# Long convolution beside a gated matmul: who turns the filter's rows, and over how much work the convolution is spread

## The chip, the cores and the metric

The kernel runs on one core of a Trainium2 chip. The metric is the device time of one execution in microseconds (us), lower is better. The engines named below are PE (matmuls; PEld is its weight load), DVE (element by element), ACT (copies and functions), POOL and SP; POOL, SP and ACT also issue the transfers (DMAs), each from its own in-order queue.

## The reference, cut to what matters

The forward result is `x + s * silu(B)`, with x of 2048 rows by 1024 columns in bf16, `xn` its layer norm, `s` a long convolution and `B` a gated matmul; then all gradients.

```python
xn = _layernorm(x)
# s: shift convolution with 4 taps, product, long causal convolution by FFT, gate
kv = shift(k, shift_k) * v
y  = irfft(rfft(pad(kv)) * rfft(pad(ssm_k)))[:S] + kv * ssm_D     # ssm_k: 1024 x 2048
s  = xn * y
# B: gated matmul, F = 3584
B  = ((xn @ w_gate) * (xn @ w_up)) @ w_down
out = x + s * silu(B)          # and the vector-Jacobian product for ten inputs
```

`ssm_k` is the long filter: one row of 2048 taps for each of the 1024 channels.

## The kernel before, in words

**Layout.** The 2048 rows of the sequence are split by a half c (2), a row u (128) and a residue r (8): row = 1024 c + 8 u + r. A tile with u on the 128 partitions holds sixteen blocks (c, r). The Fourier transform of length 4096 is done as matmuls over u (tables TF, TI) and as sums over r on DVE. The 1024 channels go in eight slices ds of 128.

**The gate/up stage.** `gu_unit` (L629) takes four row blocks at a time of one slab of 256 columns of w_up and w_gate. For each row block PE does eight matmuls of 512 columns into `psg` (L645), of which there are two buffers, ACT copies psg out (L647), and a tick is called. DVE multiplies gate and up into `hN` (L659), PE transposes hN into `tr` (L674, one buffer), ACT copies that to `hT` (L675, two buffers), SP stores it to HTd. Fourteen slabs; the first two partly in a start-up that is not touched.

**The convolution forward** (`conv_forward`, L685) is a generator that emits work slice by slice and yields its estimated DVE cost. For each slice it transforms kv (shifted k times v, from `shift`, once for two slices) and the filter, and multiplies:

- `half` (L764) does the matmuls of a half transform into `psF` (L235, two buffers) and ACT copies them to `SP`.
- `transform` (L771) does the sums on DVE; kind 0 is kv for ds > 0, kind 1 the filter. The list EIGHT picks the eight-residue form for slices 0 and 7.
- `h_rows(ds, c)` (L722) makes the filter's rows ready: `load_h` has brought the slice's 128 channels by 2048 taps into the lower half of U[5] (`hrow`, channels on partitions, tap order c, u, r). For each r PE transposes every eighth tap (L731, L733), eight transposes into `tr`, and ACT copies the eight blocks to `hx` with a scale (L734). It is called for slice ds + 1 in the middle of slice ds's kind 1 transform, once for each c. The next slice's transform reads hx.
- `product` (L333) multiplies the spectra, `inv_dft` or `inv8` brings the product back into HX on DVE, and `tail` (L743) does the last matmuls into `psY` (L438 or L449), from where ACT copies to `yf` and POOL stores to YFd.

`shift` uses U[7] for its products.

**The pace.** `make_pump` runs the generator up to a given share of F_TOTAL. `tick` (L916) is called after each row block and pumps to a share that grows in proportion to (count + 6.5) / (NT + 3.5), with NT = 24 * 8 + 14 = 206. The count starts at -5 and there are 200 row blocks, so it is 195 at the stage's end. DVE's instructions of the convolution keep their emitted order (`pinned`, L207); otherwise a scheduler places the instructions on each engine.

**The first pair.** With the gate/up stage done, the assertion at L981 demands that all forward transforms have been emitted, and psF's space is given to `psbm`. `bm_first` (L973) does 28 chunks fc for the first two row blocks of `h @ w_down` (L969): 112 matmuls of 512 columns. After fc = 5, 7, ... 27 it calls `tick(0.74)`. Between the first four chunks and the rest, pools are released and opened: `ub` holds U[8] to U[11], `bw` and `mh` hold later tiles. Then the loads of the last three down weights (`load_wd(4..6)`, L1252) and of the next pair's operand (`load_ht(1)`) are issued, and `drain` empties the generator. `gate` (L1187) does the elementwise work of each row block on ACT and DVE; it reads YFd. Row block accumulators use three PSUM tiles in turn.

The rest of the kernel (seven more pairs, then all gradients) is bound to the same engines in other ways and isn't edited.

Of the kernel before, what the change touches and what calls it, by code (L numbers as in the profile page):

```python
# [10 lines left out]
ACT = mybir.ActivationFunctionType  # L11
ALU = mybir.AluOpType
AX = mybir.AxisListType
BF16 = mybir.dt.bfloat16
# [5 lines left out]
def build_kernel(  # L20
# [11 lines left out]
    nc = tc.nc  # L32
    P = 128
# [3 lines left out]
    NB = S // P  # L37
    DC = D // P
    NF = F // P
# [3 lines left out]
    WSC = 2.0 / 2048.0  # L43
# [16 lines left out]
    def ld(out, in_):  # L60
        return nc.sync.dma_start(out=out, in_=in_)
# [182 lines left out]
    def net(w):  # L244
        w -= 0.95 * pe_us[0]
        pe_us[0] = 0.0
        return w
# [12 lines left out]
    def fwd4_buf(wp):  # L260
        return wp.tile([P, 2, 2, 4, 256], F32, name="W", tag="W")
# [242 lines left out]
    U = [ua.tile([P, 4096], BF16, name=f"U{i}") for i in range(8)]  # L504

    def u8(i, pat="p (a x) -> p a x", **kw):
        return U[i][:].rearrange(pat, **kw)
# [170 lines left out]
    h_out = []  # L678
# [1 line left out]
    INV8 = (2, 4, 6)  # L680
    SHIFT_W = 8 * 2.3

    conv_state = {"forward": True}

    def conv_forward():  # L685
        S_ = conv_state
# [11 lines left out]
        def load_h(ds):  # L698
            hrow = U[5][:, 0:2048].rearrange("p (c u r) -> p c u r", c=2, r=8)
            cld(U[5][:, 0:2048], A_ssm_k[ds * P:(ds + 1) * P, :])  # L700
            S_["h", ds] = hrow
# [20 lines left out]
        def h_rows(ds, c):  # L722
            if ds == 8:
                return
            hrow = S_["h", ds]
            if c == 0:
                S_["hx"] = cf.tile([P, NB, P], BF16, name="hx")
            pe_us[0] += 0.47
            ps = ps_tr.tile([P, 8, P], BF16, name="tr")
            with tc.issue_after(tr_ln[0].ins):  # L730
                nc.tensor.transpose(ps[:, 0, :], hrow[:, c, :, 0], ident[:])  # L731
            for r in range(1, 8):
                nc.tensor.transpose(ps[:, r, :], hrow[:, c, :, r], ident[:])  # L733
            nc.scalar.activation(S_["hx"][:, 8 * c:8 * c + 8, :], ps[:], ACT.Copy, scale=WSC)  # L734
            if c == 1:
                h_out.append(ds)
                if ds + 1 < 8:
                    load_h(ds + 1)

        def kvs(ds):  # L740
            return S_["kvt", ds // 2][:, :, ds % 2 * P:(ds % 2 + 1) * P]
# [18 lines left out]
        cf = pool("cf", 1)  # L760
# [9 lines left out]

        def transform(ds, kind, sp, X, C, ahead, step):  # L771

            if (ds, kind) in EIGHT:
                W = fwd4_buf(cs)[:].rearrange("p a b c x -> p (a b c) x")
                for n, w in enumerate(fwd8(sp, X, W, C, ahead)):
                    if n in (0, 2, 4, 6):
                        step()
                    yield net(w)
                return
            W = fwd4_buf(cs)  # L780
            fwd4_sums(W, sp[0], 0)
# [12 lines left out]
            yield net(2.4)  # L794
# [9 lines left out]
        for ds in range(8):  # L804
            yield 0.5
            if ds % 2 == 1 and ds < 7:
                with tc.issue_after(S_["kst"].ins):
                    for c in range(2):
                        load_kv(ds // 2 + 1, c)
            D0 = Dz[:, ds * P:(ds + 1) * P]  # L810
            sph = []
            KX = cx.tile([P, 16, 256], BF16, name="KX")
            HX = cs.tile([P, 16, 256], BF16, name="HX", bufs=2)
            own_room = lambda X: X[:].rearrange("p a x -> p (a x)").bitcast(F32).rearrange("p (a x) -> p a x", a=8)[:, 0:4]
            eight = (ds, 1) in EIGHT
            if ds == 0:
                yield from transform(0, 1, sp, HX, own_room(KX), lambda i: sph.append(half(0, kvs(0), i)), nop)
            else:
                yield from transform(ds, 0, sp, KX, own_room(HX), lambda i: sph.append(half(ds, S_["hx"], i, D0)), nop)
                S_["kst"] = st(KFd[ds], KX[:])  # L820
            next(tl, None)
            room = cf.tile([P, 4, 256], F32, name="room", tag="hx")[:] if eight else None
            yield from transform(ds, int(ds > 0), sph, HX if ds else KX, room, nop1 if eight else lambda c: h_rows(ds + 1, c),
                                 lambda: next(tl, None))
            if ds == 0:
                S_["kst"] = st(KFd[0], KX[:])
            if eight:
                h_rows(ds + 1, 0)
            turned(HX, 1, 0, 1)
            yield 1.3  # L830
            if eight:
                h_rows(ds + 1, 1)
            if ds == 7:
                cf.release()
                S_["forward"] = False
            st(HFd[ds], HX[:])
            yield from product(KX, HX, KX, cs, False, 0)
            if ds % 2 == 1 and ds < 7:
                yield from shift(ds // 2 + 1)
            sp = []  # L840

            def ahead():
                if ds < 7:
                    sp.append(half(ds + 1, kvs(ds + 1), len(sp)))
            yield from (inv8 if ds in INV8 else inv_dft)(KX, HX, cs, ahead if ds % 2 == 0 else None, ahead)
            if ds % 2 == 1:
                ahead()
            S_["G", ds] = HX
            tl = tail(ds)
# [27 lines left out]
    last, root, xst = layer_norm(*xs[0])  # L877
    xsts = [xst]
    for i, (b0, n, x4) in enumerate(xs):
        chunk[0] = i  # L880
        if i + 1 < len(xs):
            with tc.issue_after(last.ins):
                last, root, xst = layer_norm(*xs[i + 1])
# [27 lines left out]
    ps_cv = pool("ps_cv", 2, space=PSUM)  # L911
    pump, drain = make_pump(conv, F_TOTAL)
    cnt = [-5]
    NT = 24 * 8.0 + 14

    def tick(by=1):  # L916
        cnt[0] += by
        if cnt[0] == -4:
            pump((SHIFT_W + 4.05) / F_TOTAL)
        if cnt[0] >= -2:  # L920
            pump((SHIFT_W + (F_TOTAL - SHIFT_W) * (cnt[0] + 6.5) / (NT + 3.5)) / F_TOTAL)

# [26 lines left out]
    for hf in range(2):  # L949
# [5 lines left out]
        for sl in range(NSL - 2, NSL):  # L955
            for b0 in (8 * hf, 8 * hf + 4):
                gu_unit(sl, b0, 4, slabs[sl - NSL + 2], tick)
            if (hf, sl) == (1, NSL - 2):
                wd_ld = load_wd(3)
# [13 lines left out]
    def bm_first(fcs):  # L973
        for fc in fcs:
            for i in range(2):
                mm = bm_mm(pss[i], lambda fc: HT0[fc // 16][:, fc % 16], i, fc)
            if fc % 2 == 1 and fc > 4:
                tick(0.74)
        return mm

    assert not conv_state["forward"]  # L981
# [4 lines left out]
        flush()  # L986
    for p_ in (ps_gu, fg, fw):
        p_.release()

    ub = pool("ub", 1, side="right")
    U += [ub.tile([P, 4096], BF16, name=f"U{i}") for i in range(8, 12)]
    bw = pool("bw", 2, side="right")
    mh = [pool("mh0", 1, side="right")]
    ps_bx = pool("ps_bx", 1, space=PSUM)
# [181 lines left out]
    bpump, bdrain = make_pump(conv_backward(), C_TOTAL)  # L1179

    ddo = const.tile([P, 8], BF16, name="ddo")
    WD += [u8(j, a=4) for j in (2, 3, 9)]
    DBMT = [u8(q, a=DC) for q in (10, 8, 4, 5)]

    tr_name = ["tr"]
# [44 lines left out]
        return wdt  # L1230

    def load_ht(bp):
        if bp == 1:
            two_ = [u8(10, a=16), u8(8, a=16)]
            for f0, f1 in ((0, 16), (16, 24), (24, 28)):
                last = ld(two_[f0 // 16][:, f0 % 16:f0 % 16 + f1 - f0], ht_rows(bp, f0, f1))
            return (lambda fc: two_[fc // 16][:, fc % 16]), last
        ht = mh[bp % 2].tile([P, NF, 256], BF16, name="ht")
        for f0, f1 in ((0, 24), (24, 28)):
            last = ld(ht[:, f0:f1], ht_rows(bp, f0, f1))  # L1240
        return (lambda fc: ht[:, fc]), last
# [7 lines left out]
            ld(t, GUd[k // 2, k % 2])  # L1249
            DGU[k] = t  # L1250

    for j in range(4, 7):  # L1252
        wd_ld = load_wd(j)
    with tc.issue_after(wd_ld.ins):
        ht1 = load_ht(1)
    with tc.issue_after(ht1[1].ins):
        ht2 = load_ht(2)
    bm_first(range(4, NF))
    drain()
    PIN[0] = False  # L1260
    mh.append(pool("mh1", 1, side="right"))
# [93 lines left out]
    def load_h(sl):  # L1355
        h = u8(HSL[sl % 3], "p (a b f) -> p a b f", a=2, b=NB)
        ld(h, Hd[sl])
        hs[sl] = h
# [64 lines left out]
    for k in range(NSL - 1):  # L1423
# [19 lines left out]
        for f in range(2):  # L1443
# [7 lines left out]
            f0 = k * SLW + f * P  # L1451
# [180 lines left out]
```

## Time and profile before

| what | value |
|---|---|
| median of 3 runs | 1929.33 us (1928.45 to 1930.34) |
| profiled execution, its own time | 1929.26 us |
| its span, first to last instruction | 1927.5 us |
| granted TensorE clock, mean | 1.000 |
| PE idle in the span | 15.6 us (1927.5 - 1911.9) |
| gate/up stage, paced part | some 70 to 518 us |
| first pair of row blocks | 518 to 545 us |

How to read it: the page gives busy time by engine, then the span in 40 slices (48 us each) with a digit for the busy tenths. Answers of the trace give waits (who waited for whom, total us, times, longest), busy time in chosen stretches, and timelines (start, duration, engine, line, what). A line such as `psF<-kv,TF` names the tile written and the tiles read. PE's matmuls are pipelined: their durations overlap, and work is better counted by the distance between their starts.

### The profile page before, as it was taken

Reading aid. Unit: us, or ns where it says so; the run is one execution under the profiler, and the core shown is the slowest. Engines: PE = TensorE matmul, PEld = TensorE weight load, DVE = VectorE, ACT = ScalarE, POOL = GpSimd, SP = SyncE. Lnnn points to the kernel's source line nnn. Section 1 sums busy time; section 2 is a strip of 40 time slices with the busy share of each in tenths; the row PEclk is TensorE's granted clock in tenths of the full one; section 3 lists DMA queues with packets and bytes.
Section 4 is the critical chain, followed back from the end, with each engine's and each line's share of the span. In section 5 each row is a group of like instructions: output and inputs, shape, how many; then the busy total and the mean of one; then the engine's idle time right before and its main releaser. Section 6 shows DMA issues by size and latency. Waiting matters only on the chain.

```text
span 1927.5 us, 27456 instructions
## 1 busy us (share of the span) xinstructions
PE 1911.9 (99%) x10978; PEld 1030.1 (53%) x10978; DVE 1542.5 (80%) x1695; ACT 638.7 (33%) x943; POOL 331.0 (17%) x461
## 2 busy tenths in 40 slices
PE   8999999999999999999999999999999999999999
PEld 5555555555444456665666666664444444444444
DVE  8999999999937555888899999999996404287884
ACT  5854555555432233343222322222222102011113
POOL 5121212111112210000122131021211101011111
PEclk9999999999999999999999999999999999999999
DMA  9776866758899987666788698575786999889975
GB/s 297 264 259 221 257 211 229 234 197 266 270 278 312 298 291 257 209 201 218 264 243 264 234 247 263 201 262 186 224 253 174 143 205 217 168 178 188 189 180 171
DMA packets 451360, 444.43 MB, mean 231 GB/s; under 512 B 268800, under 2 KB 371612, under 8 KB 436768
## 3 DMA queue, kind: packets, MB, share of 16 engines
q1 hardware_dynamic: 394848, 243.36, 47.9%
q0 software_dynamic: 40064, 169.95, 27.6%
q10 hardware_dynamic: 16320, 29.36, 4.2%
q8 instruction: 86, 1.41, 0.3%
q14 instruction: 42, 0.34, 0.1%
HBM read 194.00 MB, written 185.64 MB: 197 GB/s over the span
## 4 chain that ended last, share of the span: by engine, by line
PE 80%; DVE 15%; issue 3%; DMA 1%; ACT 1%; SPq 0%; POOL 0%; DVEq 0%; ACTq 0%; POOLq 0%
PE psb L1340 20%; PE psx L1470 20%; PE psb L1323 10%; PE psbm L969 10%; PE psb L1418 9%; PE psg L645 6%; DVE W L213 4%; DVE KX L213 3%; DVE HX L213 2%; DVE m L213 2%; PE psF L235 1%; DVE U L213 1%; DVE hN L213 1%; PE psY L438 1%; PE psY L1116 1%
## 5 line engine op out<-in xcount | busy, mean ns | idle before, releaser
L645 PE MATMUL psg<-wslab,U 128*128 128x512 bf16 x1792 | 407.2, 379 | 2.5 <-DMA wslab<-in_B_w_gate_dram 1.6
L1340 PE MATMUL psb<-U,U 128*128 128x512 bf16 x1792 | 397.1, 379 | 0.0
L1470 PE MATMUL psx<-U,dgut 128*128 128x512 bf16 x1536 | 332.8, 379 | 0.0
L1470 PEld LDWEIGHTS <-dgut 128*128 128x128 bf16 x1792 | 175.3, 98 | 211.4
L1340 PEld LDWEIGHTS <-U 128*128 128x128 bf16 x1792 | 175.2, 98 | 198.0
L645 PEld LDWEIGHTS <-U 128*128 128x128 bf16 x1792 | 172.5, 98 | 187.7 <-issue 2.3
L1323 PE MATMUL psb<-wdt,U 128*128 128x256 bf16 x1792 | 205.6, 273 | 0.0
L1323 PEld LDWEIGHTS <-U 128*128 128x128 bf16 x1792 | 175.3, 98 | 29.2
L1418 PE MATMUL psb<-U,U 128*128 128x512 bf16 x816 | 177.1, 379 | 0.0
L213 DVE TENSOR_TENSOR W<-W 128x1024 f32<-128x1024 f32 (+1 forms) x174 | 171.6, 1003 | 3.7
L1345 ACT CAST wb<-psb 128x512 bf16<-128x512 f32 x112 | 65.6, 586 | 315.1 <-PE psb L1340 313.4
L969 PE MATMUL psbm<-U,ht 128*128 128x512 bf16 x672 | 145.7, 379 | 0.0
L1418 PEld LDWEIGHTS <-U 128*128 128x128 bf16 x896 | 87.5, 98 | 104.5
L647 ACT CAST gut<-psg 128x512 bf16<-128x512 f32 x156 | 91.6, 588 | 119.4 <-PE psg L645 118.9
L1502 ACT ACTIVATE dx_t<-dxn 128x1024 bf16<-128x1024 f32 x15 | 15.9, 1057 | 324.6 <-DVE dxn L213 324.6
L1168 DVE SCALAR_TENSOR_TENSOR dkp<-dkT,kT 128x1024 bf16<-128x1024 bf16 (+2 forms) x64 | 78.4, 1224 | 38.9 <-DMA dkT<-DKSHd 36.9
L969 PEld LDWEIGHTS <-ht 128*128 128x128 bf16 x672 | 65.6, 98 | 78.6
L213 DVE TENSOR_TENSOR U<-U,dht 128x2048 bf16<-128x2048 bf16 x56 | 68.3, 1221 | 46.8 <-ACT dht L1325 46.7
L1325 ACT CAST dht<-psb 128x512 bf16<-128x512 f32 x112 | 65.7, 587 | 116.3 <-PE psb L1323 116.3
L66 POOL DMA_DIRECT2D Hd<-hN x54 | 37.3, 691 | 297.5 <-DVE hN L213 295.0
L213 DVE TENSOR_TENSOR dxn<-psx,dxna_t 128x1024 f32<-128x1024 f32 x15 | 18.3, 1222 | 78.2 <-PE psx L1470 73.3
L1449 ACT CAST wbs<-psb 128x512 bf16<-128x512 f32 x51 | 29.9, 586 | 145.7 <-PE psb L1418 134.2
(237 smaller groups left out, 2452.0 us busy)
## 6 DMA issues: line engine op xcount, KB each, us to landing
U<-GUd SPq DMA_DIRECT2D x28, 1024.0 KB, 8.2
DGd<-U SPq DMA_DIRECT2D x28, 1024.0 KB, 5.8
GUd<-gut ACTq DMA_DIRECT2D x39, 512.0 KB, 5.7
out_dram<-wb SPq DMA_DIRECT2D x112, 128.0 KB, 4.0
U<-Hd SPq DMA_DIRECT2D x14, 1024.0 KB, 6.0
Hd<-hN POOLq DMA_DIRECT2D x54, 256.0 KB, 4.2
HTd<-hT SPq DMA_DIRECT2D x52, 256.0 KB, 4.1
ht<-HTd SPq DMA_DIRECT2D x6, 1536.0 KB, 10.1
```

The lines of the kernel that those rows point to most:

```text
L66: ins = nc.gpsimd.dma_start(out=out, in_=in_)
L213: pinned(V.tensor_tensor(o, a, b, op))
L645: gu_mm[0] = nc.tensor.matmul(ps[:], XNT[q][:, dc, qi * P:(qi + 1) * P], w[:, dc].rearrange("p a f -> p (a f)"), start=(dc == 0), stop=(dc ...
L647: nc.scalar.copy(out=gut[:, :, i], in_=ps[:].rearrange("p (a f) -> p a f", a=2))
L969: mm = nc.tensor.matmul(ps[:, dh * 512:(dh + 1) * 512], ht(fc)[:, i * P:(i + 1) * P], WD[fc // 4][:, fc % 4, dh * 512:(dh + 1) * 512], sta ...
L1168: ins = V.scalar_tensor_tensor(prod[:].rearrange("p r d -> p (r d)")[:, lo:H], dkT[:, 0, lo:H], 1.0, kT[:, 0, 13 + m + lo:13 + m + H], op0 ...
L1323: nc.tensor.matmul(ps[:, x * SLW:(x + 1) * SLW], DBMT[2 * hf + g][:, dc, (b % 4) * P:(b % 4 + 1) * P], wdt[:, dc, :], start=(dc == 0), sto ...
L1325: nc.scalar.copy(out=dht[:, 2 * e:2 * e + 2].rearrange("p b f -> p (b f)"), in_=ps[:])
L1340: nc.tensor.matmul(ps[:], XN[b // 4][:, b % 4, dc * P:(dc + 1) * P], dgus[b // 8][:, :, b % 8], start=(b == 0), stop=(b == NB - 1))
L1345: nc.scalar.copy(out=wb[:, dc % 2].rearrange("p a f -> p (a f)"), in_=ps[:])
L1418: nc.tensor.matmul(ps, h[:, f, b, :], DBM[b // 4][:, b % 4, dh * 512:(dh + 1) * 512], start=(b == 0), stop=(b == NB - 1))
L1470: nc.tensor.matmul(ps[:, dh * 512:(dh + 1) * 512], t[n][:, f, i * P:(i + 1) * P], WGU[n][:, f, dh * 512:(dh + 1) * 512], start=(n == 0 and ...
```

## The change

Three parts go together. From the second slice on, `h_rows` does not use PE: ACT reads the filter's rows from U[5] with a step of eight taps and writes them, scaled and in the order c, r, u, into the lower half of U[7]; after the second half SP issues one transposing DMA of that 128 x 2048 tile into hx. Slice 0 keeps the transposes. The convolution is paced over NT = 24 * 8 + 20 ticks; all fourteen odd chunks of the first pair tick by a whole 1. And the flag that allows psF's space to be reused is set when slice 7's last transform begins, not when it ends; a second flag, `filters`, still marks its end, and the code does chunks of the first pair until it is reached before the pools that need the convolution's space are opened. The loads of the last down weights and of the second pair's operand are issued ahead of that loop.

```diff
-    conv_state = {"forward": True}
+    conv_state = {"forward": True, "filters": True}
...
             hrow = S_["h", ds]
+            if ds > 0:
+                by_r = U[7][:, 0:2048].rearrange("p (c r u) -> p c r u", c=2, r=8)
+                nc.scalar.activation(by_r[:, c], hrow[:, c].rearrange("p u r -> p r u"), ACT.Copy, scale=WSC)
+                if c == 1:
+                    S_["hx"] = cf.tile([P, NB, P], BF16, name="hx")
+                    nc.sync.dma_start_transpose(out=S_["hx"][:], in_=U[7][:, 0:2048])
+                    h_out.append(ds)
+                    if ds + 1 < 8:
+                        load_h(ds + 1)
+                return
...
         def transform(ds, kind, sp, X, C, ahead, step):
+            if ds == 7 and kind == 1:
+                S_["forward"] = False
...
                 cf.release()
-                S_["forward"] = False
+                S_["filters"] = False
...
-    NT = 24 * 8.0 + 14
+    NT = 24 * 8.0 + 20
...
-            if fc % 2 == 1 and fc > 4:
-                tick(0.74)
+            if fc % 2 == 1:
+                tick()
...
     U += [ub.tile([P, 4096], BF16, name=f"U{i}") for i in range(8, 12)]
+    WD += [u8(j, a=4) for j in (2, 3, 9)]
+    for j in range(4, 7):
+        wd_ld = load_wd(j)
+
+    def load_ht1():
...
+    with tc.issue_after(wd_ld.ins):
+        ht1 = load_ht1()
+    fc_ = 4
+    while conv_state["filters"]:
+        bm_first([fc_])
+        fc_ += 1
     bw = pool("bw", 2, side="right")
...
-    for j in range(4, 7):
-        wd_ld = load_wd(j)
-    with tc.issue_after(wd_ld.ins):
-        ht1 = load_ht(1)
...
-    bm_first(range(4, NF))
+    bm_first(range(fc_, NF))
```

`load_ht1` has the body that `load_ht` had for its second pair.

More of the change, by code (lines that the diff above doesn't have):

```diff
@@ L994, in build_kernel @@
     U += [ub.tile([P, 4096], BF16, name=f"U{i}") for i in range(8, 12)]
+    WD += [u8(j, a=4) for j in (2, 3, 9)]
+    for j in range(4, 7):
+        wd_ld = load_wd(j)
+    def load_ht1():
+        two_ = [u8(10, a=16), u8(8, a=16)]
+        for f0, f1 in ((0, 16), (16, 24), (24, 28)):
+            last = ld(two_[f0 // 16][:, f0 % 16:f0 % 16 + f1 - f0], ht_rows(1, f0, f1))
+        return (lambda fc: two_[fc // 16][:, fc % 16]), last
+    with tc.issue_after(wd_ld.ins):
[4 more added lines that the diff above has]
+        fc_ += 1
     bw = pool("bw", 2, side="right")
@@ L1181, in build_kernel @@
     ddo = const.tile([P, 8], BF16, name="ddo")
-    WD += [u8(j, a=4) for j in (2, 3, 9)]
     DBMT = [u8(q, a=DC) for q in (10, 8, 4, 5)]
@@ L1232, in load_ht @@
     def load_ht(bp):
[L1233 to L1237, printed above, removed]
         ht = mh[bp % 2].tile([P, NF, 256], BF16, name="ht")
```

## The prediction

> **What bounds the kernel now.** I read the span in slices first, then the waits of TensorE, then busy time by stretch, then single stretches of the timeline. The page says that PE never rests and that DVE is as full as PE in the first quarter of the span only:
>
> ```profile
> PE 1911.9 (99%) x10978; PEld 1030.1 (53%) x10978; DVE 1542.5 (80%) x1695; ACT 638.7 (33%) x943; POOL 331.0 (17%) x461
> ...
> PE   8999999999999999999999999999999999999999
> ...
> DVE  8999999999937555888899999999996404287884
> ```
>
> A busy PE is modelled, so I also took the distance from one matmul's start to the next: 0.216 us for 512 columns, 0.109 us for 256, 0.056 us for a 128-column transpose. From 60 to 560 us nothing else shows except three gaps. They are the whole list of waits of PE in that stretch:
>
> ```profile
> PE psF L235 <- DVE kv L213: 3.1, 2, 1.9
> PE tr L674 <- DVE hN L213: 1.7, 1, 1.7
> ```
>
> So in this stage two engines run neck and neck, and PE is stopped where it catches up with DVE. By stretch (columns: PE, PEld, DVE, ACT, POOL, clock, DMA share, GB/s):
>
> ```profile
> 300.00:400.00 100.00, 99.82 (x632) 56.76 (x631) 99.07 (x89) 56.37 (x81) 18.86 (x26) 1.00 0.71 231
> 400.00:425.00 25.00, 23.12 (x145) 13.31 (x144) 24.76 (x18) 13.32 (x18) 2.61 (x4) 1.00 0.64 208
> 475.00:500.00 25.00, 23.25 (x137) 12.20 (x136) 24.79 (x33) 13.60 (x21) 2.98 (x6) 1.00 0.82 269
> 525.00:550.00 25.00, 25.00 (x134) 12.83 (x133) 4.39 (x3) 2.91 (x6) 0.02 (x1) 1.00 0.83 225
> ```
>
> DVE is 99% busy up to 525 us, then rests for over 20 us while PE does the first pair of row blocks (L969): that is the room the change wants to use. The clock is 1.00 throughout. After 550 us PE has no wait worth naming, so what is won before 550 us should reach the end.
>
> **Removed: fourteen halves of eight transposes.** In the timeline of PE around slice 7 (start, duration, what):
>
> ```profile
> 433.25 0.22 PE L731 MATMUL tr<-ident,U 128*128 128x128 bf16 x1
> 433.30 0.60 PE L733 MATMUL tr<-ident,U 128*128 128x128 bf16 x7
> 433.74 1.67 PE L645 MATMUL psg<-wslab,U 128*128 128x512 bf16 x7
> 435.25 0.22 PE L731 MATMUL tr<-ident,U 128*128 128x128 bf16 x1
> 435.31 0.61 PE L733 MATMUL tr<-ident,U 128*128 128x128 bf16 x7
> 435.75 2.54 PE L645 MATMUL psg<-wslab,U 128*128 128x512 bf16 x11
> ```
>
> From the group's first start to the next L645 matmul is 0.49 and 0.50 us. Seven slices times two halves times 0.50 is 7.0 us. The matmul ahead of a group is also followed later than usual (0.22 to 0.50 us where 0.216 is normal); over the fourteen halves that adds 0.8 us. **7.8 us** of PE's queue goes, all of it in the stage where PE is full.
>
> **Moved: the pace of the convolution.** The pump releases convolution work in proportion to (ticks + 6.5) / (NT + 3.5). At the last matmul group of the gate/up stage the count is 195, so the share released falls from 201.5/209.5 = 0.962 to 201.5/215.5 = 0.935. F_TOTAL works out to some 408, so about 10 us of DVE work moves out of the stage into the first pair, and all along the stage DVE owes less at each PE position. Is that enough? I summed, along the order in which the instructions stand in each program, PE's start distances up to a matmul that reads DVE's result, and DVE's start distances (medians by shape from this trace) up to the instruction that makes it. PE's sum minus DVE's, before and after, in us:
>
> - kv of slice 2: 173.8 - 177.0 = -3.2; after 177.0 - 177.6 = -0.6
> - kv of slice 4: 285.2 - 289.9 = -4.7; after 290.4 - 291.1 = -0.7
> - kv of slice 6: 396.6 - 403.3 = -6.7; after 405.4 - 403.9 = +1.5
> - worst hN transpose: 474.5 - 482.8 = -8.3; after 463.4 - 465.0 = -1.6
> - last slice's inverse, read by L449: after 519.9 - 520.9 = -1.0
>
> The first, -3.2, passed without a wait in the trace (PE had lost that much more in its start-up). Each further step down, 1.5, 2.0 and 1.6, is a stall, against 1.2, 1.9 and 1.7 us of idle time in the trace: the bookkeeping gives the three waits, so I trust it for the changed order. There nothing lies below -3.2. **4.8 us** of stalls (3.1 + 1.7) goes.
>
> **What is late next.** DVE's last inverse step ends at 529.4 us now (its timeline: start 527.06, two instructions, 2.36). The four tails that read it (L449) start at 541.96 us now, at 525.1 in PE's sum. In the changed order they stand behind all 112 matmuls of the pair instead of 104, at 519.9. That is 541.96 - 5.2 - 4.8 - 0.8 = 531.2 us, 1.8 us behind DVE. DVE will no longer be always late, so it will itself wait for some SP copies: the tightest, kv of slice 6, has 1.8 us of room today and its sum falls from 9.6 to 2.1 while PE's lag shrinks by 6, which is a wait of 1 to 1.5 us. I leave **0.6 us** of PE waiting at the tails. Behind them the gates wait for YFd's round trip as now; pair 2's accumulators are needed only some 14 us later, and ht1's loads and the last down weights (issued at 530 us now, the second read at 540) keep their place relative to PE.
>
> **Added on ACT.** The fourteen copies of L734 (1.02 us, from PSUM, contiguous) become fourteen from SBUF that pick every eighth element. No ACT row reads with such a step. Nearest in engine and size is L734 itself, 1.02 us; the same rows read with that step slowed PE's weight load from 98 to 148 ns, a factor of 1.5, giving 1.53; POOL's reordering at L1120, 4.15 us for 2048 elements, gives 2.07 for 1024.
>
> ```profile
> L733 PEld LDWEIGHTS <-U x112: 142/148/155, 63.5 to 435.6; 128*128 128x128 bf16 x112
> ...
> L734 ACT ACTIVATE hx<-tr x16: 1016/1024/1042, 65.2 to 436.0; 128x1024 bf16<-128x1024 bf16 x16
> ...
> L1120 POOL COPY ho<-yl x8: 3731/4147/4683, 1252.5 to 1489.6; 128x2048 bf16<-128x2048 bf16 x8
> ```
>
> In the built order both copies stand side by side for slices 1, 3, 4 and 7. With two psg buffers ACT may hold the queue for 2 x 1.73 - 2 x 0.59 = 2.3 us before PE stops (a group of eight is 1.73 us, its copy 0.59). Two at 1.02 fit and cost nothing; two at 1.53 cost 0.8 us, at 2.07 1.8 us, so 3.1 or 7.4 us over four slices. I take 1.02, the row of the same engine and size, and keep 7.4 for the range. A gain is excluded, since ACT is 56% busy here and bounds nothing. The copies' wait for U[7] is behind the shift's last product, which ACT has already passed when it copied the same slice's kv spectrum.
>
> The Trainium skill speaks against this part: SBUF — State Buffer, Door 1: The DMA port swizzle, says that an access which crosses to a new 16-byte line pays a penalty, and eight bf16 is just such a line. The weight load's 148 against 98 ns agrees with it; it names no size for ACT, so by it the sum would lie somewhere in my upper half.
>
> **Added on SP and the DMA engines.** Seven transposes of 512 KB. The row of the same size is wdt, from DRAM:
>
> ```profile
> L1229 SPq DMA_TRANSPOSE wdt<-in_B_w_down_dram x14: 1307/4266/7498, 652.4 to 1203.1; - x14
> ...
> DMA to landing us min/median/max: 4.2/7.9/16.0
> ```
>
> None reads SBUF, so I keep 1.3 to 10.0 us on SP (the longest transpose row, at L1404) and 4 to 16 us to land. hx is read 26 to 49 us after today's PE transposes, so the landing is hidden; the shortest distance, 26 us, is slice 1's, and only 10 + 16 us together would reach it. The queue they are put into carries the hT stores and the slabs. hT has two buffers and a copy every 7.4 us, so a store may end 14.7 us after its copy; behind a 4.3 us transpose and with 4.1 us of its own it ends after 8.4, behind 10.0 after 14.1. Both fit. Seven times 512 KB is 3.7 MB in a stretch that moves some 105 MB at a DMA share of 0.7: nothing.
>
> **Sum.** The profiled execution took 1929.3 us (span 1927.5 and 1.8 around it), as the median of the runs shown, 1929.3. 7.8 + 4.8 - 0.6 = 12.0, so **1917.3 us**, 0.6% faster.
>
> **Rivals.** (1) *DVE comes late at the tails.* It has 1.8 us of room. If each of seven slices loses one copy's 1.0 us because SP's spectrum copy stands behind a reordering copy, DVE ends 7 us later, PE waits 5.2 us, and the time is 1922. For it: DVE is 99% busy and has no reserve. Against: the tight SP copies are those of kv, and the reordering stands behind them. (2) *The gain is eaten.* Copies at 2.07 us (7.4 us) together with the late DVE (5.2 us) give 1930: no change. POOL's row speaks for it; against it, the two prices have to come together. (3) *SP is held, slower.* If a transpose out of SBUF holds SP longer than any row shows, the hT store behind it is late, ACT stops at the next hT copy, and with it the psg copies. ACT stops from 14.7 - 4.1 = 10.6 us of issue, PE from 12.9, and the gain is gone at 12.9 + 12/7 = 14.6 us. At twice the longest row, 19.9 us, PE loses 7.0 us seven times: 1966. Against: SP spends 367 us of waiting for hT, so it is mostly free; for: no row has this source.
>
> **Chances.** Forecast 0.57, rival 1 0.19, rival 2 0.10, rival 3 0.14. The forecast itself spans 1914 (8.2 + 5.3 + 1 for the runs' spread, no new wait) to 1920 (copies at 1.53). To leave out no more than 2 in 10 the range takes in rival 1 and the dear copies alone (1924.7), with the runs' spread: 1913.5 to 1926.5. Faster by over 0.2%, about what a measurement of this kernel can tell from no change (below 1925.5): 0.76; within it 0.10; slower 0.14.
>
> **What would show it.** L733 falls from 112 to 14 matmuls; PE waits for kv and hN vanish and PE's busy time drops by 7 to 8 us; the first psbm matmul, at 518.4 us now, starts near 506; the 525 to 550 stretch has DVE no longer resting from its start relative to the pair; the reordering copies take 1.0 us; the transposes take 4 us on SP. Wrong would be: a copy of 2 us or more, psF waiting for hx, L645 waiting for ACT, hT copies waiting for a store, or L449 waiting for HX by more than 2 us.

## The result, and the profile after

The changed kernel takes 1956.47 us (median of 4 runs, 1955.83 to 1962.85), the kernel before 1928.93 on the same chip: 1.0151 times, interval 1.0138 to 1.0163. Where 12 us less were forecast it is 27.5 us more. The profiled execution has a span of 1954.1 us, 26.6 more than before.

The page of the changed kernel, the lines that answer to those of before. PE has lost 112 transposes and yet is busy longer, and ACT does not show what it did: 33% before and after.

```profile
PE 1917.2 (98%) x10866; PEld 1026.5 (53%) x10866; DVE 1542.9 (79%) x1695; ACT 652.9 (33%) x943; POOL 329.2 (17%) x461
...
PE   8999999999999999999999999999999999999999
...
DVE  8989899898968554888799899999997303488873
```

PE's waits from 60 to 600 us (who waits for whom, total us, times, longest). The waits for DVE (two lines before, for kv and for hN) are gone, as forecast. In their place PE waits eight times for ACT, to take over an accumulator (`psg`, `psY`):

```profile
PE psg L645 <- ACT gut L647: 9.6, 3, 4.7
PE psg L645 <- ACT U L647: 8.2, 3, 4.6
PE psY L449 <- ACT yf L759: 8.0, 2, 4.9
```

By stretch (PE, PEld, DVE, ACT, POOL, clock, DMA share, GB/s), the same four as before:

```profile
300.00:400.00 100.00, 92.89 (x552) 51.76 (x551) 87.89 (x77) 57.16 (x74) 16.94 (x24) 0.95 0.66 207
400.00:425.00 25.00, 25.00 (x143) 12.53 (x142) 24.83 (x22) 11.48 (x19) 3.76 (x5) 1.00 0.82 278
475.00:500.00 25.00, 25.00 (x143) 12.77 (x141) 24.73 (x25) 10.33 (x16) 2.74 (x5) 1.00 1.02 338
525.00:550.00 25.00, 25.00 (x143) 12.80 (x141) 24.33 (x34) 11.26 (x18) 4.27 (x6) 1.00 0.69 216
```

Between 300 and 400 us PE does 552 instructions where it did 632, DVE is 88% busy where it was 99%, and the clock is 0.95 on average. So both engines that ran neck and neck now stand still for something else.

**Where the 26.6 us lie.** The first `psbm` matmul starts at 518.4 us before and at 545.0 after: all of the difference, since from there to the end both take 1409.1 us. Up to there, by the distance of matmul starts: stops of over 0.3 us grow from 5.3 us (three) to 27.1 us (eight), +21.8. After most of them the granted clock is 0.5 for 3.4 or 6.8 us, 30.7 us in six stretches, in which the starts of 512-column matmuls lie 0.43 us apart and not 0.216; I sum the excess to 12.7 us. The transposes' 7.8 us are gone. 21.8 + 12.7 - 7.8 = 26.7, which is 0.2 more than the start of `psbm` moved.

Seven of the eight stops stand where the seven pairs of copies stand in ACT's queue. The eighth, 3.0 us at 500 us, does not: the last copy started at 439.54, and here ACT had waited for the store of an hT buffer:

```profile
501.39 1.01 ACT L675 COPY hT<-tr 128x1024 bf16<-128x1024 bf16 x1 [5.42 <-DMA HTd<-hT]
```

One stop, read in two timelines (start, duration, engine, what, in brackets the idle time before it and what ended it). ACT first, then PE:

```profile
105.28 0.59 ACT L647 CAST U<-psg 128x512 bf16<-128x512 f32 x1 [1.14 <-PE psg L645]
105.76 1.02 ACT L675 COPY hT<-tr 128x1024 bf16<-128x1024 bf16 x1
111.23 2.02 ACT L728 ACTIVATE U<-U 128x1024 bf16<-128x1024 bf16 x1 [4.46 <-DMA hx<-U]
113.15 0.57 ACT L647 CAST U<-psg 128x512 bf16<-128x512 f32 x1
113.62 2.03 ACT L728 ACTIVATE U<-U 128x1024 bf16<-128x1024 bf16 x1
```

```profile
105.52 3.62 PE L645 MATMUL psg<-wslab,U 128*128 128x512 bf16 x16
113.78 4.48 PE L645 MATMUL psg<-wslab,U 128*128 128x512 bf16 x13 [4.64 <-ACT U L647]
```

A reordering copy for slice 2 stands in ACT's queue at 107 us, though its rows go on only at 146.37, when the next transposing DMA is issued. It may not write U[7] yet: the transposing DMA of slice 1's rows, issued at 104.65, still reads it. That one had itself waited on SP for the space of hx: in slice 0 DVE works there (a tile `room` has the same place), and its last instruction on it ended at 104.62. The six later ones go out when the last matmul that reads hx has ended (0.03 us after it). ACT waits 4.46 us and works 2.02; both psg buffers fill in the meantime, and PE stands. The clock of the stretch behind it, and of the one behind the stop at 342 us:

```profile
105.00:109.00 4.00, 4.00 (x26) 2.02 (x24) 4.00 (x6) 1.50 (x2) 1.78 (x3) 1.00 0.94 165
109.00:114.00 5.00, 0.36 (x2) 0.10 (x1) 3.10 (x3) 2.77 (x3) 0.00 (x0) 0.95 1.04 420
114.00:117.00 3.00, 3.00 (x8) 1.06 (x7) 0.85 (x2) 2.12 (x2) 0.00 (x0) 0.52 0.33 135
...
347.00:352.00 5.00, 4.61 (x15) 2.16 (x15) 0.21 (x1) 3.43 (x4) 1.15 (x1) 0.50 0.18 57
```

The fourteen copies together, what ended ACT's idle time before them, and SP's transposing DMAs:

```profile
L728 ACT ACTIVATE U<-U x14: 1997/2060/2140, 83.1 to 439.5; 128x1024 bf16<-128x1024 bf16 x14
...
  DMA hx<-U: 9.2, 3
  DVE U L213: 6.8, 3
```

```profile
L731 SPq DMA_TRANSPOSE hx<-U x7: 1417/2037/3033, 104.7 to 466.5; - x7
...
DMA to landing us min/median/max: 4.3/5.3/6.9
```

A copy takes 2.06 us, twice what I took, and its queue place costs ACT another 16.0 us of waits. The transposing DMAs, 1.4 to 3.0 us on SP, lie near the cheap end of my bounds.

### The profile page after: what moved, and what is told of

Same layout as the page of the kernel before. It is cut to its first block, busy times and chain, and to the rows that moved or that the text cites. A ratio compares the mean times of both kernels' runs of the same rounds, so it can differ in the third digit from the quotient of the medians.

```text
span 1954.1 us, 27246 instructions
## 1 busy us (share of the span) xinstructions
PE 1917.2 (98%) x10866; PEld 1026.5 (53%) x10866; DVE 1542.9 (79%) x1695; ACT 652.9 (33%) x943; POOL 329.2 (17%) x461
## 4 chain that ended last, share of the span: by engine, by line
PE 85%; DVE 7%; DMA 3%; issue 2%; ACT 2%; POOL 0%; SPq 0%; ACTq 0%; DVEq 0%; POOLq 0%
PE psb L1354 20%; PE psx L1484 20%; PE psg L645 10%; PE psb L1337 10%; PE psbm L981 10%; PE psb L1432 9%; PE psF L235 2%; DVE U L213 2%; DVE KX L213 1%; DVE W L213 1%; DMA HTd<-hT 1%; DMA hx<-U 1%; DVE m L213 1%; ACT U L728 1%; PE psY L438 1%
## 5 line engine op out<-in xcount | busy, mean ns | idle before, releaser
L645 PE MATMUL psg<-wslab,U 128*128 128x512 bf16 x1792 | 417.0, 386 | 20.8 <-ACT gut L647 10.2
L213 DVE TENSOR_TENSOR W<-SP 128x1024 f32<-128x1024 f32 x64 | 74.4, 1219 | 14.0 <-ACT SP L257 10.9
```

The source lines that it names most:

```text
L213: pinned(V.tensor_tensor(o, a, b, op))
L645: gu_mm[0] = nc.tensor.matmul(ps[:], XNT[q][:, dc, qi * P:(qi + 1) * P], w[:, dc].rearrange("p a f -> p (a f)"), start=(dc == 0), stop=(dc ...
```

## The experiments

Two theories. **A**: ACT is the cause: the copies' length and their waits hold its queue, and the stops halve the clock. **S** (the prediction's third rival): SP and the transfers are the cause, through hT's stores. The first two expectations also name **B**, the later pace is the cause, and C, which is S under an earlier name. Edits are against the changed kernel, ratios against the kernel before with their intervals.

**1. The parts alone.** First the pace with PE's transposes kept for every slice:

```diff
-            if ds > 0:
+            if ds > 8:
```

> All filter rows are again transposed by PE, the pace over 212 ticks, the early release of psF's space and the loop of the first pair stay. Theory A (the loss is ACT's: reordering copies of 2.06 us that also stand in its queue waiting for U[7], PE stops, and its clock falls to half after the long stops): no reordering, so no loss; the wait list of PE shows no psg waits on ACT, the clock stays 1.000, the waits for kv and hN (4.8 us) shrink, and the time is 1922 to 1927 us. Theory B (the loss is the later pace: tails, gates or the pair come late): the loss stays, 1945 us or more. Theory C (the transposing DMAs hold SP's queue or load the DMA engines): as A.

Measured 1924.28 us, 0.9971 (0.9959 to 0.9982). Of PE's waits from 60 to 580 us one line is left; before it was 3.1 + 1.7:

```profile
PE psY L438 <- ACT yf L759: 0.4, 1, 0.4
```

`psbm` starts at 512.9, 5.5 us earlier, against 4.8 forecast for this part. Then the turning alone:

```diff
-    NT = 24 * 8.0 + 20
+    NT = 24 * 8.0 + 14
...
-            if fc % 2 == 1:
-                tick()
+            if fc % 2 == 1 and fc > 4:
+                tick(0.74)
```

> ACT and the DMA turn the rows as in the changed kernel, but the pace is that of before (206 ticks, twelve ticks of 0.74 in the first pair). Theory A: the stops by ACT stay (22 us of idle, some 12 us of half clock), 7.8 us of transposes stay away, so 1948 to 1960 us. Theory B: back near 1922 us, for the pace was the fault. Theory C: as A.

Measured 1948.18 us, 1.0093 (1.0076 to 1.0110). So the turning does the harm. The parts do not add up: with it the new pace makes things 8.3 us worse (1956.5 against 1948.2), without it 5.1 us better. PE's wait for hN is still there (2.8 us), the two for kv are not: a stop by ACT gives DVE time, so that there is little left for the pace to win. In the two profiled runs `psbm` starts 7.0 us apart; 1.8 us of that are stops (27.1 against 25.3) and 4.9 half clock (30.7 us of it against 20.5). Why the later pace meets more half clock was not tested; three stops of the earlier pace, of 2.4 to 3.2 us from start to start, passed at full clock (the last section has to do with this).

**2. ACT or SP.** Without the copies; the DMA turns U[5] as it lies:

```diff
-                nc.scalar.activation(by_r[:, c], hrow[:, c].rearrange("p u r -> p r u"), ACT.Copy, scale=WSC)
...
-                    nc.sync.dma_start_transpose(out=S_["hx"][:], in_=U[7][:, 0:2048])
+                    nc.sync.dma_start_transpose(out=S_["hx"][:], in_=U[5][:, 0:2048])
```

> The changed kernel without ACT's fourteen copies: the transposing DMA reads the rows as they lie in U[5], so order and scale of the filter are left out and the run is for its time alone. ACT is then free of the new work, and SP and the DMA engines carry all of theirs. Theory A (ACT is held by the copies, their 2.06 us and their 16 us of waits for U[7], and the stops cost half clock on top) expects 1917 to 1923 us: the run with the pace alone, 1924.3, less the 7.8 us of transposes, plus up to 6 us for the tails. Theory S (the seven transposing DMAs are slow among the other transfers and hold SP, so that an hT copy on ACT waits for its store) expects 1928 to 1945 us, with ACT hT waiting for HTd in stops of 5 us and more.

And the copies without a use, PE transposing as before (`return` and the DMA are taken out of the branch, so that it falls through to the transposes):

```diff
-                if c == 1:
-                    S_["hx"] = cf.tile([P, NB, P], BF16, name="hx")
-                    nc.sync.dma_start_transpose(out=S_["hx"][:], in_=U[7][:, 0:2048])
-                    h_out.append(ds)
-                    if ds + 1 < 8:
-                        load_h(ds + 1)
-                return
```

> PE transposes all slices as in the kernel before, with the changed pace (1924.3 us), and ACT does the fourteen stepped copies into U[7] besides, which nothing reads; no transposing DMA. Theory A expects 1935 to 1950 us: fourteen times 2.06 us in ACT's queue, pairs of them at 4.1 us against the 2.3 us that ACT may hold PE's two psg buffers, and a wait for the shift's products of some 7 us; stops over 2.3 us draw half clock. Theory S expects no more than 1930 us, since no transfer is added.

Measured 1921.13 us, 0.9949 (0.9930 to 0.9969), and 1949.66 us, 1.0094 (1.0070 to 1.0118). For the changed kernel this decides for A: seven transposing DMAs on SP and no copies, 3.2 us less than the pace alone; fourteen dead copies and no transposing DMA, 25.4 us more. PE's waits without the copies, then with the dead copies:

```profile
PE psg L645 <- ACT gut L647: 3.6, 1, 3.6
PE psF L235 <- ACT SP L295: 0.2, 1, 0.2
PE psF L235 <- ACT SP L257: 0.2, 1, 0.2
```

```profile
PE psg L645 <- ACT gut L647: 13.4, 6, 4.7
PE psg L645 <- ACT U L647: 5.8, 5, 3.2
```

The dead copies wait as well, 6.3 us for the shift's products and 3.9 for the load of the rows, so the 25.4 us are not length alone.

**3. Why the copies are dear: length.** Contiguous copies at the same place (order left out):

```diff
-                nc.scalar.activation(by_r[:, c], hrow[:, c].rearrange("p u r -> p r u"), ACT.Copy, scale=WSC)
+                nc.scalar.activation(U[7][:, 1024 * c:1024 * c + 1024], U[5][:, 1024 * c:1024 * c + 1024], ACT.Copy, scale=WSC)
```

> The changed kernel, but ACT copies the rows in the order they lie (contiguous read and write, the reordering is left out, so the filter's values are wrong); place, waits and transposing DMAs are as in the changed kernel. If the length of the stepped copy is the main fault: copies of 1.0 us, two of them fit the 2.3 us that are free, and the time falls to 1918 to 1930 us. If the wait for U[7] (16 us in ACT) is the main fault: ACT still stops for it, and the time stays at 1938 us or more, with the clock still falling to half after three to five stops.

And a contiguous read with a stepped write (128 elements):

```diff
-                nc.scalar.activation(by_r[:, c], hrow[:, c].rearrange("p u r -> p r u"), ACT.Copy, scale=WSC)
+                nc.scalar.activation(by_r[:, c].rearrange("p r u -> p u r"), hrow[:, c], ACT.Copy, scale=WSC)
```

> The changed kernel, but ACT reads the rows in order and writes with a step of 128 elements, so the same reordering is done on the writing side. Theory A with a dear read: the copies take 1.0 us, ACT is held for 2 us less per slice, the waits for U[7] stay (16 us), and the time lies between 1935 and 1950 us. If a stepped write costs as much as a stepped read, the copies take 2 us and the time stays near 1956 us.

Measured 1939.78 us, 1.0048 (1.0035 to 1.0062), and 1991.44 us in a single run, above both values expected for it. The copies' group in the one and in the other:

```profile
L728 ACT ACTIVATE U<-U x14: 1039/1057/1090, 85.4 to 427.5; 128x1024 bf16<-128x1024 bf16 x14
...
  DMA hx<-U: 9.5, 3
  DVE U L213: 6.8, 3
```

```profile
L728 ACT ACTIVATE U<-U x14: 4745/4766/5088, 83.2 to 474.6; 128x1024 bf16<-128x1024 bf16 x14
```

A contiguous copy takes 1.06 us, as long as the L734 row, and its waits stay. Of the 35.3 us between the changed kernel and the one without copies, the step (14.0 us of ACT time) makes 16.7 us and the contiguous copies in that queue place 18.6 us. The 18.6 hold the contiguous copies' own time as well as their 16.3 us of waits; the runs don't part these two.

**4. Why they are dear: place.** Odd slices' turned rows go to the upper half of U[7], to part the DMA from hx:

```diff
-                    S_["hx"] = cf.tile([P, NB, P], BF16, name="hx")
+                    S_["hx"] = U[7][:, 2048:4096].rearrange("p (b u) -> p b u", b=NB) if ds % 2 else cf.tile([P, NB, P], BF16, name="hx")
```

> The changed kernel, but the odd slices' turned rows go into the upper half of U[7] and only the even ones into hx, so no transposing DMA waits for the slice in use. Stepped copies of 2.06 us stay. Theory A: SP is no longer held for hx, ACT's three waits for the DMA (9.2 us) go, its waits for the shift (6.8 us) stay, and so do stops from two copies in a row; 1938 to 1950 us. If only the length counts: no change, 1956 us. If only waiting counts: 1935 us or less.

Measured 1961.05 us, 1.0149 (1.0122 to 1.0177), above all that was expected. The run counts for its time alone, for with this edit the filter's values come out wrong. The copies of slices 2, 4 and 6 came 10 to 14 us earlier (97, 205 and 332 us against 111, 216 and 343), and the copies' wait for the DMA grew from 9.2 to 21.6 us. Then the copies held back behind ACT's last copy of the filter's half transform, so that U[7] and hx are free when they come up:

```diff
...
-                nc.scalar.activation(by_r[:, c], hrow[:, c].rearrange("p u r -> p r u"), ACT.Copy, scale=WSC)
+                with tc.issue_after(S_["hxcp"].ins):
+                    nc.scalar.activation(by_r[:, c], hrow[:, c].rearrange("p u r -> p r u"), ACT.Copy, scale=WSC)
...
```

(The lines left out set `hxcp` to that last copy.)

> The changed kernel, but ACT's reordering copies are ordered behind ACT's copies of the same slice's filter spectrum (the readers of the hx buffer in use), so they come when U[7] is free and the transposing DMA behind them finds hx free. Theory A: ACT's waits for hx and for the shift (16 us) go to near nothing, two copies still hold ACT for 4.1 us where 2.3 are free, PE stops stay under 2 us each, the clock stays at 1.00, and the time is 1915 to 1926 us. Theory C: nothing moves, above 1945 us. If length alone were the fault and not the place: 1940 us or more.

The same with contiguous copies (order left out):

> Late copies (behind ACT's copies of the same slice's filter spectrum) and contiguous (the reordering is left out, the filter's values are wrong). Theory A: neither wait nor length is left, the stops at psY (11.9 us in the late run) go too, since a copy of 1.0 us holds ACT no longer than the copy of before did. 1914 to 1922 us, the forecast's sum. If the late run's single stop of 8.4 us comes from the transposing DMA beside other transfers, it can appear here as well, and then 1925 to 1935 us.

Measured 1947.83 us, 1.0089 (1.0061 to 1.0117), and 1945.05 us, 1.0072 (1.0051 to 1.0092). Both lie above what A expected. The copies' 16 us of waits went to nothing in both, and most of the time did not come back: here theory S comes in. In the second, SP's queue (start, duration) and ACT:

```profile
371.20 0.37 SPq L541 DMA_DIRECT2D wslab<-in_B_w_up_dram  x1
371.62 1.42 SPq L541 DMA_DIRECT2D wslab<-in_B_w_gate_dram  x1
373.15 12.92 SPq L733 DMA_TRANSPOSE hx<-U  x1
386.16 2.33 SPq L61 DMA_DIRECT2D HTd<-hT  x2
```

```profile
405.52 1.01 ACT L676 COPY hT<-tr 128x1024 bf16<-128x1024 bf16 x1 [14.59 <-DMA HTd<-hT]
```

One transposing DMA held SP for 12.92 us, the hT stores stood behind it and landed late, ACT waited 14.59 us for an hT buffer and PE stood 13.3 us. That is the third rival's chain, but not its price: by its bounds PE stops only from a hold of 12.9 us. What it left out is the landing. The hT stores behind this DMA took 18.9 us from issue to landing (median), where those of the kernel before take 4.1; first the row of before, then the two of this run:

```profile
HTd<-hT SPq DMA_DIRECT2D x52, 256.0 KB, 4.1
```

```profile
HTd<-hT SPq DMA_DIRECT2D x2, 256.0 KB, 18.9
hx<-U SPq DMA_TRANSPOSE x1, 27.8
```

In the first of the two runs the hold is only 6.2 us and PE's stop still 8.4: the stores behind it landed after 21.6 and 18.9 us. PE there also waits 11.9 us in twelve pieces for ACT to empty psY, which contiguous copies bring down to almost nothing.

Two more ways to relieve ACT's queue did not help. The order made by POOL:

```diff
-                nc.scalar.activation(by_r[:, c], hrow[:, c].rearrange("p u r -> p r u"), ACT.Copy, scale=WSC)
+                nc.gpsimd.tensor_scalar(by_r[:, c], hrow[:, c].rearrange("p u r -> p r u"), WSC, None, op0=MUL)
```

> The changed kernel with the stepped copies done by POOL (a scaled copy, some 2.1 us per half by POOL's own reordering row) and not by ACT. Theory A: ACT never waits for U[7], PE has no psg wait on ACT and the clock stays at 1.00: 1914 to 1925 us. POOL's waits for U[7] and hx then hold POOL's stores (Hd, KFd, YFd) and the next filter load; if these are what hurts, PE waits for hN's buffers and the time is above 1930 us.

Measured 1950.33 us, 1.0097 (1.0069 to 1.0126). POOL takes 4.2 us for a half and DVE is slowed beside it: DVE's sums, 2289 ns before, take 2729 on average, and PE waits 20.1 us for ACT's copies of the half transforms, which wait for DVE's sums (27.7 us). Before, then in this run:

```profile
L213 DVE TENSOR_TENSOR W<-KX 128x2048 f32<-128x2048 bf16 x16 | 36.6, 2289 | 0.3
```

```profile
L213 DVE TENSOR_TENSOR W<-KX 128x2048 f32<-128x2048 bf16 x16 | 43.7, 2729 | 0.3
```

And the copies in four pieces, each right behind a psg copy:

```diff
...
+            gut_cp[0] = nc.scalar.copy(out=gut[:, :, i], in_=ps[:].rearrange("p (a f) -> p a f", a=2))
+            if pieces:
+                pieces.pop(0)()
...
```

> The changed kernel with each slice's reordering cut into four pieces of 512 elements (some 1.05 us each by half of 2.06), each put in ACT's queue right behind a psg copy, where ACT has some 1.1 us of rest before the next. Theory A expects 1916 to 1925 us, since no piece holds ACT for long and none stands ahead of its slice. Theory S expects 1930 to 1945 us as in the two runs with late copies (1947.8 and 1945.1), with the same stop of 8 us and more where ACT hT waits for HTd near 390 us.

Measured 1947.76 us, 1.0076 (1.0047 to 1.0105), with single runs from 1931.8 to 1967.8: inconclusive. The last slice's pieces came so late that they were written over a tile of w_down in U[7], whose load ACT awaited for 9.7 us; the time contains a stop of 9.5 us for that, so it tells neither theory from the other. The other ACT waits of this profile speak for S: 30.4 us in eight times for hT's stores.

**5. Is the transposing DMA dear by itself?** Everything is computed again, without ACT and PE: the DMA turns the rows on their way in, and a store and a load through DRAM put them in order; the filter's scale goes into the copies of the half transforms.

```diff
...
+                nc.sync.dma_start_transpose(out=raw, in_=A_ssm_k[ds * P:(ds + 1) * P, :])
...
+                st(RWd[ds + 1].rearrange("(b p) x -> p b x", p=P), raw)
...
+                    ld(S_["hx"][:].rearrange("u (c r) x -> u c (r x)", c=2),
+                       RWd[ds].rearrange("(c u r) x -> u c (r x)", c=2, u=P))
...
```

> The changed kernel with neither PE nor ACT putting the filter's rows in order: SP's transposing DMA brings a slice's rows from the input, channels turned into taps, into the lower half of U[5] (in the place of load_h's plain load); POOL stores the tile to DRAM, and SP loads hx from there in the order c, r, u (256 B written, 2 KB read at a time). The scale goes into ACT's copies of the filter's half transforms, which are there already, so ACT gets no instruction more. Everything is computed. Theory A (only ACT's copies spoiled the change) expects 1918 to 1924 us, as without the copies (1921.1), and below the pace alone (1924.3); no stop of PE over 2 us before 460 us. Theory S (seven more transposing DMAs beside the stage's other transfers hold SP and make hT's stores late) expects 1930 to 1945 us, with ACT hT waiting for HTd for 10 us and more.

Then the transposing DMA tied behind the load of hx, and then, for slice 7 alone, behind the next slab's loads:

```diff
...
+                        with tc.issue_after(hx_ld.ins):
+                            load_h(ds + 1)
...
```

> As the run that does everything by DMA (1942.2), but the transposing DMA of a slice's rows is put behind the load of hx for the slice before it, where the first had let SP issue it up to two slices ahead, beside the loads of k and v (one such took 10.55 us on SP at 121 us and PE stood for 14.6 us behind it). Everything is computed. If it is the place that made the transposing DMA slow: 1919 to 1926 us, with no stop of PE over 2 us between 90 and 460 us. If a transposing DMA is liable to hold SP wherever it stands: 1930 us and more, with ACT hT waiting for HTd again.

> As the tied DMA run (1924.9), with one thing exchanged: the transposing DMA of slice 7's rows stands on SP behind the next slab's two loads (1 MB) and not ahead of them. In the traces so far the transposing DMA for slice 7 took 12.9, 14.8 and 6.2 us on SP where it stood behind these loads (the three runs with late copies), and 2.0 and 4.4 us where it stood ahead of them (without copies, and tied). If the order on SP is what counts: 8 to 15 us on SP for this one, a stop of PE near 390 us, and 1932 to 1942 us. If not: under 6 us on SP, and 1923 to 1927 us.

Measured 1942.20 us, 1.0069 (1.0053 to 1.0086), which lies in S's range; 1924.89 us, 0.9974 (0.9962 to 0.9985); 1923.25 us, 0.9968 (0.9955 to 0.9980). Left free, the scheduler sent the transposing DMAs out up to two slices ahead, one of them beside the loads of k and v: 10.55 us on SP, and a stop of 14.6 us. Tied, they take 3.0 to 5.1 us on SP and PE has one stop of more than 1.2 us (3.85 us at 466). Behind the slab's loads slice 7's hold grows from 4.35 to 8.50 us,

```profile
372.85 8.50 SPq L712 DMA_TRANSPOSE U<-in_A_ssm_k_dram  x1
```

and the time does not. The hT stores behind it landed after 11.1 and 9.2 us, ACT waited 1.7 us for one and PE not at all. So a hold of 8.5 us cost nothing here where one of 6.2 us had cost a stop of 8.4: what differs is how late the stores land. The order on SP counts for the hold, but doesn't alone make the 12.9. Last, the late copies with contiguous reads and the next rows' load moved away from the transposing DMA:

```diff
...
-                        load_h(ds + 1)
+                        S_["next_h"] = ds + 1
...
+            if "next_h" in S_:
+                with tc.issue_after(newest_cp[0].ins):
+                    load_h(S_.pop("next_h"))
```

> As the late copies with the order left out (1945.1; the filter's values are again not in order), but the next slice's rows are loaded into U[5] some 10 us later, behind the product of the spectra, so that load no longer runs beside the transposing DMA. In the run without copies the load had to wait for the transposing DMA anyway, and no transposing DMA took over 3.8 us on SP; here one took 12.9. If the load beside it is what made it slow: the stop of 13 us near 393 us goes, and the time is 1924 to 1932 us. If other transfers (the spectrum's store and the slabs) do it: the stop stays, 1938 to 1948 us.

Measured 1949.71 us, 1.0100 (1.0084 to 1.0116), with 14.75 us on SP. The edit failed to do what it was for: the load still went out at 374.50 us, 0.1 us after the transposing DMA. Which neighbour (that load, the spectrum's store, the slabs) makes a transposing DMA out of SBUF that slow, and the stores behind it slow to land, stays open.

## Why the prediction was wrong, point by point

- **Removed transposes, 7.8 us, and stalls, 4.8 us:** right. The pace alone moved `psbm` forward by 5.5 us, 0.7 more than the stalls; with the transposes gone and no copies it starts at 510.3. 518.4 - 7.8 - 5.5 is 505.1; a new stop of 3.7 us, 1.3 us lost to half clock behind it and 0.2 more in small stops make 510.3. Take the copies away and the forecast is 3.8 us off (1921.1 against 1917.3).
- **What is late next, "0.6 us of PE waiting at the tails":** wrong in kind. No wait at the tails shows without the copies. The next limit is hT's store at 465 us, behind a slab, two down weights and a load of HTd on SP's queue, at a DMA share of 1.05. As I read it, PE came there earlier, those transfers became no shorter, and ACT waited; with the pace alone ACT waits 0.7 us there. The changed kernel's eighth stop, at 500 us, stands at the same place in the work. SP first, then ACT, in the run without copies:

```profile
448.67 19.59 SPq L61 DMA_DIRECT2D HTd<-hT  x3
```

```profile
466.87 1.01 ACT L675 COPY hT<-tr 128x1024 bf16<-128x1024 bf16 x1 [6.15 <-DMA HTd<-hT]
```

- **Added on ACT, the step that failed, first in a size:** I took 1.02 us from the row of the same engine and size. It measured 2.06, the upper bound I had kept (POOL's 2.07). The tie was the wrong one: L734 reads one contiguous run, and what decided was the step, which the weight load's factor of 1.5 on the same rows had already shown. The Trainium skill's SBUF — State Buffer, Door 1: The DMA port swizzle, told of the penalty that I weighed and set aside, without a size; here it is a factor of 1.95 (2060 against 1057 ns) for a read with a step of 16 bytes, and 4.5 (4766) for a write with a step of 256; no other step was run.
- **Then in the claim "The copies' wait for U[7] is behind the shift's last product, which ACT has already passed":** wrong, and by the split of 16.7 and 18.6 us the larger half, with the reserve made there. Three copies waited 6.8 us for that product, and three waited 9.2 us for a reader that the text does not name: the transposing DMA of the slice before, which itself waits on SP until hx's space is free. A PE transpose stood where PE's queue put it; a copy with no input from PE may stand anywhere, and the scheduler put them 17 to 49 us ahead of the transposing DMA that takes their rows on. I read the built order for which copies are neighbours, not for what must have happened by then.
- **And in the price of a stop:** fourteen copies at 2.07 were to cost 7.4 us by two psg buffers' slack. Alone, with no transposing DMA, they cost 25.4. The slack was reckoned for pairs that start at once, and for the one such pair the reckoning is near (slice 1's: a stop of 1.4 us, where 1.8 was reckoned). For the others the waits come on top, all seven pairs stop PE and not four, and most longer stops are paid again in clock: 12.7 us in the changed kernel. The trace of before could not show this, its stops of up to 1.9 us pass at clock 1.00.
- **Rival 2 ("the gain is eaten", 1930)** had half of the mechanism, the copies at 2.07 us, whose 7.4 us became 35. Its other half, the late DVE, did not come: no wait of PE for DVE is left. **Rival 3** is not what happened in the changed kernel (a transposing DMA holds SP for 1.4 to 3.0 us; the one wait of 5.4 us for hT's store and its stop of 3.0 us come some 29 us behind the last of them), but its chain did happen when other things moved: 12.9 us on SP, a stop of 13.3 us, once and not seven times. Its bounds were wrong, for they took a store to land in 4.1 us.
- **DMA bytes and landing, "hidden":** right in place and size (4.3 to 6.9 us to land), except that the landing holds U[7], and through it ACT.
- **Two readings that nothing rests on:** the page shows DVE as full as PE also in ten slices in the middle of the span, not in the first quarter only; and 1929.3 - 14.5 is 1914.8, not 1914.

## What to carry to other kernels

Work taken off a full engine and given to one that is half idle is not free if that engine also empties the full one's buffers: price the new instruction by its access pattern (step, not only size), ask for every buffer it writes who read it last and when, and see where a scheduler may put it once it has lost its tie to the old engine. Spreading the convolution's pace won 5 us by itself; the turning as changed lost all of it and more, and done by DMA alone, tied to its place, brings next to nothing (1923.2 to 1924.9 against 1924.3), because the transfers at 465 us are the next limit: of some 7 us that PE was spared, a stop of 3.7 us there and some 1.6 us of half clock behind it take most.

## What the runs showed of the hardware that was not expected

- In the changed kernel the granted clock was 0.5 for 3.4 or 6.8 us after six of eight stops, the shortest 2.33 us (from start to start); it was not after the stops of 1.47 and 2.68, and with the dead copies not after two of 3.5. Length alone doesn't decide it, but the place does. The six half-clock stretches begin at 113.47, 219.28, 314.86, 345.58, 441.15 and 502.59 us, whole multiples of 3.413 us apart (the first two 31 of them), and in each case the 3.413 us just ahead hold 2.2 us or more of stop. The stop of 2.68 lies across a boundary of this grid, with 1.6 us before it and 0.9 behind; the two of 3.5 likewise in their run, 1.4 + 1.9 and 1.9 + 1.5.
- The Trainium skill, TensorE: Matmul & The Clock Gate, Part 1: The HAM clock gate, has the clock halved after an idle window of about 3.4 us that runs free of the kernel. The grid of 3.413 us agrees; but here a window that stood still for two thirds of its time was enough.
- ACT reading every eighth bf16 takes 2.06 us for 128x1024 against 1.06 contiguous; writing every 128th, 4.77.
- POOL, reading with that step, takes 4.2 us, twice the 2.07 that its L1120 row gave, and DVE's sums beside it 19% longer.
- A transposing DMA of 512 KB out of SBUF lands in 4.3 to 6.9 us in the changed kernel, and took 27.8 and 28.6 us, in the two runs with late contiguous copies, beside a slab's loads, the next rows' load and the stores of a spectrum and of YFd.
